# Moving three of the weight loads of an attention kernel's last stage, and its last store, to ScalarE's DMA queue

## The chip, the cores and the metric

One core of one Trainium2 chip. The time is the device time of one execution in microseconds. Nearly all executions of this kernel agree within 0.1%; a run counts as fast when it is within 1.5% of the fastest of its kernel. The profile is of one execution; its span, from the first to the last instruction, is about 1.8 us shorter than the timed figure.

Some words used below. A load has landed when all 16 DMA engines have reported their share of it. The granted clock is the share of TensorE's full clock that the trace records; "half clock" means a record of 0.5. An eviction copies a result of TensorE from PSUM, where matmuls leave it, to SBUF, the memory that the engines work from. A head is one of the 32 slices of wo that the output projection multiplies in turn. Times within an execution count from the first instruction of its profile.

## The reference

Grouped-query attention over a cache, for 32 sequences of 4 new tokens, with an output projection:

```python
B, Sq, D = 32, 4, 1024;  Hq, Hkv, Sk, Dh = 32, 4, 2048, 128
q = (x @ wq).reshape(B, Sq, Hq, Dh).transpose(0, 2, 1, 3)
k = repeat(k_cache, 8, axis=1);  v = repeat(v_cache, 8, axis=1)      # each 32 x 2 MiB, bf16
p = softmax(einsum("bhqd,bhkd->bhqk", q, k) * Dh ** -0.5)
o = einsum("bhqk,bhkd->bhqd", p, v)
return o.transpose(0, 2, 1, 3).reshape(B, Sq, Hq * Dh) @ wo          # wo: 4096 x 1024, 8 MiB
```

The kernel reads 151 MB and writes 0.26 MB.

## The kernel before

The kernel goes through 32 batches. All loads are issued by SyncE, in one order fixed at build time: x, four parts of wq, then k and v of the batches, then wo. Each load waits for the work that frees its slot. wo (32 heads, each 128 x 1024) comes in 14 pieces: six of 4 heads (1 MiB), two of 2, two of 1, and four halves of the last two heads.

```python
WO = (4, 4, 4, 4, 4, 4, 2, 2, 1, 1)          # heads in each piece; the last two heads come in halves
...
wo_for = [("k", B - 3), ("k", B - 2), ("k", B - 1), ("v", B - 4)]     # whose slots wo takes
...
for c, (u, m, n0, n1) in enumerate(pieces):
    ...
    p.dma("sp", lambda e, dst=dst, src=src: e.dma_start(dst, src),
        [("kt", b, 1) if kind == "k" else ("pv", b)], ("wo", c), f"s_wo{c}")
```

Every engine's program is a list in program order, so an engine's DMA issue stands between its other instructions. ScalarE's last work is the evictions of the attention output, one a batch (`o_evac`), and a third of the last copy:

```python
for i in range(B + LAG):
    j = i - LAG
    ...
    if j >= 0:
        for t in range(T):
            pe_pv(j, t)          # TensorE: attention of batch j
        ...
        o_evac(j)                # ScalarE: PSUM -> SBUF
    ...
for b0, n in ((0, 30), (30, 1), (31, 1)):
    o_turn(b0, n)                # VectorE: transpose the attention output
for u in range(Hq - 2):
    oproj(u, (0, 1, 2))          # TensorE: head u, waits for its piece of wo
...
oproj_out()                      # casts on VectorE, ScalarE, VectorE; two stores
```

## Time and profile before

| | before |
|---|---|
| time, median | 363.12 us |
| DMA queue of SyncE, share of the 16 engines | 99.0% |
| the six large loads of wo landed at | 340.6, 343.1, 345.5, 348.0, 350.5, 353.0 us |
| output projection, start of the first to end of the last matmul | 342.85 to 358.65 us |
| last piece of wo landed at | 358.2 us |

Here are lines of the page: the span, the table of DMA queues (packets, MB, share of the 16 engines' span), and the chain that ended last, by engine and by line.

```profile
span 361.4 us, 6252 instructions
...
q1 hardware_dynamic: 12240, 151.52, 99.0%
...
DMA 8%; PE 2%; SPq 1%; DVE 0%; issue 0%
DMA big<-in_wo_dram 8%; PE ps_r L394 1%; PE ps_s L420 1%; PE ps_s L16 1%; SPq L227 1%; DVE P_sb L434 0%; SPq L211 0%
```

One queue keeps the engines full, and the chain that ends last leads back to a load of wo. The chain of waits in order of time (start, duration, what) says which one:

```profile
325.16 27.84 DMA big<-in_wo_dram
...
353.04 0.39 PE ps_s L420
...
358.04 1.04 DVE P_sb L434 x2
```

A load lands at 353.0 and TensorE then works without a gap to the casts. Which load that is shows in the loads taken one by one (issue durations in ns and start of the issue; then the time from issue to landing). The first pair is the second load of wo, the second pair the sixth:

```profile
L227 SPq DMA_DIRECT2D big<-in_wo_dram x1: 432/432/432, 323.3 to 323.3; - x1
...
DMA to landing us min/median/max: 19.8/19.8/19.8
...
L227 SPq DMA_DIRECT2D big<-in_wo_dram x1: 433/433/433, 325.2 to 325.2; - x1
...
DMA to landing us min/median/max: 27.8/27.8/27.8
```

So the second load was issued at 323.3 and landed at 343.1; the sixth was issued at 325.2 and landed at 353.0. The stretches of 2 us (busy time of each engine, granted TensorE clock, DMA share, GB/s) show the stage:

```profile
core 0: us, PE busy (x) PEld busy (x) DVE busy (x) ACT busy (x) POOL busy (x), PEclk, DMA share, GB/s
...
344.00:346.00 2.00, 2.00 (x16) 0.49 (x5) 0.00 (x0) 0.00 (x0) 0.00 (x0) 1.00 0.99 410
346.00:348.00 2.00, 2.00 (x16) 0.39 (x4) 0.00 (x0) 0.00 (x0) 0.00 (x0) 1.00 1.02 426
...
350.00:352.00 2.00, 1.45 (x10) 0.39 (x4) 0.00 (x0) 0.00 (x0) 0.00 (x0) 1.00 1.00 412
352.00:354.00 2.00, 1.42 (x11) 0.29 (x3) 0.00 (x0) 0.00 (x0) 0.00 (x0) 1.00 1.00 395
...
356.00:358.00 2.00, 2.00 (x15) 0.55 (x6) 0.00 (x0) 0.00 (x0) 0.00 (x0) 1.00 0.42 144
```

TensorE starts the projection at 342.85, is full from 344 until it has caught up with the loads, and has holes at 350 to 354, where it waits for the fifth and the sixth. The DMA share falls only after 356.

### The profile page before, as it was taken

Reading aid. Unit: us, or ns where it says so; the run is one execution under the profiler, and the core shown is the slowest. Engines: PE = TensorE matmul, PEld = TensorE weight load, DVE = VectorE, ACT = ScalarE, POOL = GpSimd, SP = SyncE. Lnnn points to the kernel's source line nnn. Section 1 sums busy time; section 2 is a strip of 40 time slices with the busy share of each in tenths; the row PEclk is TensorE's granted clock in tenths of the full one; section 3 lists DMA queues with packets and bytes.
Section 4 is the critical chain, followed back from the end, with each engine's and each line's share of the span. In section 5 each row is a group of like instructions: output and inputs, shape, how many; then the busy total and the mean of one; then the engine's idle time right before and its main releaser. Section 6 shows DMA issues by size and latency. Waiting matters only on the chain. (4 is left out here: it accounts for less than half of the span.)

```text
span 361.4 us, 6252 instructions
## 1 busy us (share of the span) xinstructions
PE 307.8 (85%) x3034; PEld 147.0 (41%) x2340; DVE 269.4 (75%) x171; ACT 102.6 (28%) x110; POOL 165.4 (46%) x262
## 2 busy tenths in 40 slices
PE   1988788999989999988999888888888898889896
PEld 1002000444444555444444444443333444449711
DVE  0018799999899888879999888888888888866501
ACT  1014222333333333333333333323222233333000
POOL 8002055255555555554455444445555554444000
PEclk9999999999999999999999999999999999999999
DMA  8999999999999999999999999999999999999995
GB/s 321 433 435 432 424 424 428 435 423 424 423 428 432 428 424 430 431 430 426 424 433 428 425 428 430 430 428 426 428 432 432 426 423 435 428 426 428 413 415 215
DMA packets 12251, 151.66 MB, mean 420 GB/s; under 512 B 1360, under 2 KB 2128, under 8 KB 2768
## 3 DMA queue, kind: packets, MB, share of 16 engines
q1 hardware_dynamic: 12240, 151.52, 99.0%
q8 instruction: 6, 0.10, 0.1%
q14 instruction: 5, 0.04, 0.0%
HBM read 151.26 MB, written 0.26 MB: 419 GB/s over the span
## 5 line engine op out<-in xcount | busy, mean ns | idle before, releaser
L328 DVE STREAM_TRANSPOSE KT_sb<-big 128x2048 f32<-128x2048 f32 x64 | 146.6, 2293 | 16.7 <-DMA big<-in_k_cache_dram 16.7
L354 ACT ACTIVATE P_sb<-ps_s,negmx 128x2048 bf16<-128x2048 f32 x32 | 82.1, 2565 | 185.0 <-DVE negmx L350 185.0
L16 PE MATMUL ps_s<-KT_sb,QD_sb 128*128 128x512 bf16 x384 | 103.7, 377 | 0.0
L385 POOL COPY PD_sb<-PT_sb 32x1024 f32<-32x1024 f32 x62 | 64.1, 1034 | 63.3 <-PE ps_r L394 60.4
L385 POOL COPY big<-PT_sb 32x1024 f32<-32x1024 f32 x61 | 63.1, 1034 | 59.1 <-PE ps_r L394 56.3
L350 DVE TENSOR_REDUCE negmx<-ps_s 128x1 f32<-128x2048 f32 x32 | 73.2, 2286 | 12.4 <-PE ps_s L16 10.7
L394 PE MATMUL ps_r<-big 128*128 128x128 bf16 x1024 | 59.8, 219 | 11.4 <-PEq L85 11.4
L394 PE MATMUL ps_r<-big,PD_sb 128*128 128x128 bf16 x1024 | 59.8, 219 | 9.9 <-PEq L85 9.8
L394 PEld LDWEIGHTS ps_r<-big 128*128 128x128 bf16 x1024 | 57.9, 98 | 22.1 <-issue 21.6
L394 PEld LDWEIGHTS ps_r<-big,PD_sb 128*128 128x128 bf16 x1024 | 58.0, 98 | 21.1 <-issue 20.6
L341 PE MATMUL ps_s<-KT_sb,QD_sb 128*128 128x512 bf16 x128 | 48.3, 377 | 18.4 <-PEq L85 18.4
L341 PEld LDWEIGHTS ps_s<-KT_sb,QD_sb 128*128 128x128 bf16 x128 | 12.3, 96 | 103.1 <-issue 103.1
L363 DVE STREAM_TRANSPOSE PT_sb<-P_sb 128x1024 f32<-128x1024 f32 x32 | 39.8, 1245 | 15.8 <-ACT P_sb L354 15.8
L318 POOL COPY QD_sb<-QT_sb 32x64 f32<-32x64 f32 x128 | 29.4, 230 | 46.2 <-DVE QT_sb L297 20.5
L16 PE MATMUL ps_r<-ident 128*128 128x384 bf16 x173 | 33.3, 325 | 0.0
L366 PEld LDWEIGHTS ps_r<-ssum,permf 128*128 128x128 f32 x64 | 11.9, 187 | 24.8 <-issue 23.1
L403 ACT ACTIVATE QT_sb<-ps_r,rinv 128x128 bf16<-128x128 f32 x32 | 11.8, 367 | 29.4 <-PE ps_r L394 27.2
L279 DVE TENSOR_SCALAR KT_sb<-ps_r 128x512 bf16<-128x512 f32 x2 | 1.3, 684 | 20.3 <-PE ps_r L263 20.3
L420 PE MATMUL ps_s<-big,KT_sb 128*128 128x512 bf16 (+1 forms) x34 | 12.5, 375 | 2.0 <-DMA big<-in_wo_dram 1.2
L434 DVE CAST P_sb<-ps_s 128x512 bf16<-128x512 f32 (+1 forms) x2 | 1.0, 542 | 15.3 <-PE ps_s L420 15.3
L16 PE MATMUL ps_s<-big,KT_sb 128*128 128x224 bf16 (+1 forms) x62 | 12.0, 272 | 0.0
L252 PE MATMUL ps_r<-ident 128*128 128x384 bf16 x32 | 10.3, 322 | 0.0
(41 smaller groups left out, 85.8 us busy)
## 6 DMA issues: line engine op xcount, KB each, us to landing
big<-in_k_cache_dram SPq DMA_DIRECT2D x32, 2048.0 KB, 18.6
big<-in_v_cache_dram SPq DMA_DIRECT2D x32, 2048.0 KB, 22.1
big<-in_wq_dram SPq DMA_DIRECT2D x4, 2048.0 KB, 14.0
big<-in_wo_dram SPq DMA_DIRECT2D x6, 1024.0 KB, 22.8
big<-in_wo_dram SPq DMA_DIRECT2D x2, 512.0 KB, 24.3
big<-in_wo_dram SPq DMA_DIRECT2D x2, 256.0 KB, 22.6
big<-in_wo_dram SPq DMA_DIRECT2D x4, 128.0 KB, 17.5
P_sb<-in_x_dram SPq DMA_DIRECT2D x1, 256.0 KB, 2.6
```

What stands on the lines that cost most here:

```text
L16: return eng.add_instruction(mybir.InstMatmult(name=nc.get_next_instruction_name(), engine=eng.engine, start_tensor_calc=start, stop_tenso ...
L318: p.op("pool", lambda e, s=src, d=dst: e.tensor_copy(d, s), waits if g == 0 else [("pt", i - 2)] * (g == 1 and i > 1), ("qd", i) if g == G ...
L328: p.op("dve", lambda e, s=src, d=dst: e.transpose(d, s), waits, ("kt", i, c), gives="t_kt" if c else None)
L341: mm = lambda e, a_=(out_, lhsT, rhs), f=first, l=last: e.matmul(a_[0], lhsT=a_[1], rhs=a_[2], start=f, stop=l, skip_group_check=True)
L350: p.op("dve", lambda e: e.tensor_reduce(negmx[:, i % 4:i % 4 + 1], ps_s[:, :], AX.X, ALU.max, negate=True), [("qk", i)], ("negmx", i))
L354: p.op("act", lambda e: e.activation(P_sb[:, :, :, :].rearrange("p t r w -> p t w r"), ps_s[:, :].rearrange("p (t w r) -> p t w r", w=2, r=R),
L363: p.op("dve", lambda e: e.transpose(dst, src), [("exp", i)], ("pt", i))
L366: p.op("pe", lambda e: e.matmul(ring[(i if i == L else i // 2 * 2) % 4][:, 510 + i % 2:511 + i % 2], lhsT=permf[:, :], rhs=ssum[:, i % 4:i ...
L385: p.op("dve" if i >= B - 2 and g < i - B + 4 else "pool", lambda e, s=src, d=dst: e.tensor_copy(d, s), [free] * (g == 0 or i >= B - 2) + [ ...
L394: p.op("pe", lambda e: e.matmul(buf[:, 0:Dh], lhsT=pd_of(i)[:, t // 2, :, :, :, t % 2].rearrange("p x g q -> p (x g q)"), rhs=big[:, slot_ ...
L403: p.op("act", lambda e: e.activation(dst, src, ACT.Copy, scale=rinv[:, i % 4:i % 4 + 1]), [("pv", i), ("rinv", i)], ("o", i))
L420: mm = lambda e, a=(out_, lhsT, rhs): e.matmul(a[0], lhsT=a[1], rhs=a[2], start=(u == 0), stop=(u == Hq - 1), skip_group_check=True)
```

## The change

The intent: let a second sequencer issue part of the last loads, beside the others, and issue the two stores from two engines.

```diff
+        act_loads = []
         for c, (u, m, n0, n1) in enumerate(pieces):
 ...
-            p.dma("sp", lambda e, dst=dst, src=src: e.dma_start(dst, src),
-                [("kt", b, 1) if kind == "k" else ("pv", b)], ("wo", c), f"s_wo{c}")
+            load = ("act" if c in (1, 3, 5) else "sp", lambda e, dst=dst, src=src: e.dma_start(dst, src),
+                    [("kt", b, 1) if kind == "k" else ("pv", b)], ("wo", c), f"s_wo{c}")
+            if c in (1, 3, 5):
+                act_loads.append(load)
+            else:
+                p.dma(*load)
 ...
-                p.dma("sp", lambda e, n0=n0, n1=n1: e.dma_start(out_flat[:, n0:n1], y_sb[:, n0:n1]),
+                p.dma(("sp", "act")[j], lambda e, n0=n0, n1=n1: e.dma_start(out_flat[:, n0:n1], y_sb[:, n0:n1]),
 ...
                 o_evac(j)
+                if j == L - 1:
+                    for load in act_loads:
+                        p.dma(*load)
```

L is 31, so the three loads stand in ScalarE's program after the eviction of batch 30 and before that of batch 31.

## The prediction

> **What bounds the kernel now.** The loads. The queue table has one busy queue with 99.0% of the 16 engines' span; in the table of stretches the DMA share is 0.94 to 1.04 from 300 to 356 us, at 410 to 433 GB/s (395 and 368 at 352 to 356). So all 151 MB come one after the other. TensorE (85%) follows.
>
> The last stage, from the stretches, the timeline and the wo loads taken stretch by stretch: SyncE issues the six 1 MiB loads of wo at 322.8 to 325.2 us behind the last v load, and they land in order at 340.6, 343.1, 345.5, 348.0, 350.5 and 353.0, 2.45 us apart. The output projection starts at 342.85 (after the last transpose), runs 0.435 us for each of 32 heads, catches up with the loads at about 348 and then waits for the fifth and the sixth load (0.57 and 0.58 us). The chain of waits ends: sixth load lands 353.0, then TensorE without a gap to 358.56, casts, stores, 361.4. So the end is the landing of the sixth load plus 5.5 us. The last small pieces land at about 358.1 to 358.2, which is a second floor only 0.3 us below.
>
> **What the change does.** ScalarE's program has its three loads after the eviction of batch 30, which ran at 337.76 to 338.13, and before that of 31 (342.00). So loads 2, 4, 6 are issued at about 338.2 to 339.5 (0.43 us each, as SyncE's) instead of 323.3 to 325.2. SyncE's queue loses 3 MiB. SyncE's issues after 330.8 are today stretched to 1.2 to 6.3 us[...]; they get shorter, which is worth nothing, as these pieces were queued long before they moved.
>
> The Trainium skill, "DMA: Bandwidth & Descriptors", section "Issuing engines are not separate DMA queues", says that DMAs of all issuers run on the same 16 engines and only issue time is saved. This trace fits: engines full with one queue. Its section "Queues, rings and completion order" says that an engine takes turns between queues by packet; this trace cannot show it, having one busy queue. If so, from about 339.4 (issue plus about 1 us) both queues share 0.40 MiB/us. Estimate, equal shares: loads 1, 3, 5 land at 341.7, 346.7, 351.8; loads 2, 4, 6 at 344.4, 349.4, 353.8 to 354.4 (the earlier if ScalarE's 8 KB packets gain against SyncE's 4 KB ones). Total bytes and the end of the drain stay. Load 6 is then 0.8 to 1.4 us later, and the end follows it.
>
> The last store: ScalarE's part of the last eviction ends at 359.00, VectorE's at 359.08; SyncE issued its second store at about 359.17. ScalarE can issue at about 359.1: under 0.1 us gained.
>
> **Prediction.** 363.12 + 0.9 - 0.1 = 363.9 us; 8 in 10: 362.9 to 365.0. Faster by over 2%: 0.01; within 2%: 0.97; slower: 0.02.
>
> **What would show it.** A second queue with about 3 MB; its three issues at about 338 to 340; odd and even loads landing interleaved, the sixth at about 354; TensorE waits for loads 3 to 6 grown from 1.2 us to over 2; the drain's end unmoved; GB/s unmoved before 338.
>
> **What would make it wrong.** Two queues move more than one (each 1% of this stage is 0.2 us): slightly faster. ScalarE gets more than half: the sixth load is not late, time unchanged. ScalarE's issue blocked behind SyncE's stretched ones: the eviction of 31 and the projection start late, 1 to 3 us more. A gap in the engines' work about 333 to 339, if SyncE's queue ran empty: it holds 5 MiB then, so I expect none.

## More of the kernel before

The output projection takes the heads in order, so it needs the pieces of wo in order. The kernel also has `pe_idle(n, ...)`, which issues n matmuls whose result nobody reads, to keep TensorE busy in waits.

## The result

| | before | changed |
|---|---|---|
| median of 6 runs | 363.13 us (363.01 to 363.27) | 366.54 us (365.57 to 366.79) |
| span of the profiled run | 361.4 us | 364.7 us |
| granted TensorE clock, mean | 1.0 | 0.995 in five of six runs, 1.0 in the one of 365.57 us |
| wo, loads 1, 3, 5 landed at | 340.6, 345.5, 350.5 | 340.3, 344.0, 349.0 us |
| wo, loads 2, 4, 6 landed at | 343.1, 348.0, 353.0 | 347.8, 351.6, 355.3 us |
| last piece of wo landed at | 358.2 | 357.9 us |

The ratio is 1.0089, with a 95% interval of 1.0076 to 1.0102. A ratio here is the mean time of one kernel's fast runs over that of the other's of the same rounds, so it is not quite the ratio of the medians. By the 2% class the two are the same; but the 3.4 us are clear of the noise, and the 366.54 us lie above the prediction's range (362.9 to 365.0).

The same lines of the page, after:

```profile
span 364.7 us, 6248 instructions
...
q1 hardware_dynamic: 11664, 148.25, 95.9%
q10 hardware_dynamic: 576, 3.28, 2.2%
...
PE 9%; DMA 3%; DVE 0%; DVEq 0%; issue 0%; ACT 0%
```

The second queue is there, with 3.28 MB (three loads and a store). The chain now ends in TensorE's own work (9%) and less in DMA (3%). In order of time:

```profile
337.44 10.36 DMA big<-in_wo_dram
...
347.85 0.39 PE ps_s L425
...
348.56 0.43 PE ps_s L425
348.98 0.43 PE ps_s L16 x2
```

The load that starts the last chain is issued at 337.44 and lands at 347.80. ScalarE's loads one by one are the second load of wo (first pair) and the sixth (second pair):

```profile
L228 ACTq DMA_DIRECT2D big<-in_wo_dram x1: 402/402/402, 337.4 to 337.4; - x1
...
DMA to landing us min/median/max: 10.4/10.4/10.4
...
L228 ACTq DMA_DIRECT2D big<-in_wo_dram x1: 452/452/452, 338.4 to 338.4; - x1
...
DMA to landing us min/median/max: 16.9/16.9/16.9
```

The second load is issued at 337.4 and lands 10.4 us later, at 347.8. From there TensorE has 28 of 32 heads still to do. Its matmuls come at half the pace at first: a group of three column blocks takes 0.85 us (348.56 to 349.41) and not 0.43. The timeline shows the wait, in brackets at the end of the line:

```profile
start us, us, engine line op out<-in xcount [idle before <-releaser]
...
337.44 1.37 ACTq L228 DMA_DIRECT2D big<-in_wo_dram  x3
...
347.85 0.39 PE L425 MATMUL ps_s<-big,KT_sb 128*128 128x512 bf16 x1 [3.25 <-DMA big<-in_wo_dram]
```

The ScalarE issue of 337.44 to 338.81 runs beside the eviction and delays nothing. TensorE's projection starts at the same time as before to within 0.2 us, does the four heads of the first load, and waits 3.25 us. The stretches:

```profile
core 0: us, PE busy (x) PEld busy (x) DVE busy (x) ACT busy (x) POOL busy (x), PEclk, DMA share, GB/s
...
344.00:346.00 2.00, 0.60 (x5) 0.00 (x1) 0.00 (x0) 0.00 (x0) 0.00 (x0) 1.00 1.00 412
346.00:348.00 2.00, 0.15 (x1) 0.10 (x1) 0.00 (x0) 0.00 (x0) 0.00 (x0) 1.00 1.02 424
348.00:350.00 2.00, 2.00 (x9) 0.40 (x3) 0.00 (x0) 0.00 (x0) 0.00 (x0) 0.56 1.00 412
350.00:352.00 2.00, 2.00 (x10) 0.31 (x3) 0.00 (x0) 0.00 (x0) 0.00 (x0) 0.59 1.02 420
...
356.00:358.00 2.00, 2.00 (x15) 0.45 (x5) 0.00 (x0) 0.00 (x0) 0.00 (x0) 1.00 0.42 145
```

From 344 to 348 TensorE does 0.75 us of work. From 348 to 352 (whose TensorE columns are full only because each matmul takes longer) its granted clock is 0.56 and 0.59; the trace has one record of 0.5, from 348.2 to 351.6 us. The DMA columns have not changed: the GB/s of each stretch are within 10 of those before, and the engines run dry at the same time. So the bytes did not come later. They came in another order.

The trace's records of single DMA packets show how the queues shared the engines. By queue, in stretches of 1 us of the changed kernel:

```
us     SyncE's queue       ScalarE's queue
340    56 packets 400 KB    1 packet     8 KB
341    24 packets 176 KB   31 packets  248 KB
342    28 packets 200 KB   25 packets  200 KB
352    35 packets 110 KB   36 packets  288 KB
354   211 packets 354 KB    6 packets   16 KB
```

ScalarE's first packet starts at 341.00, and sixteen of them have started by 341.4. The first is 3.56 us after its issue began. From then on, as long as ScalarE's queue has packets for all engines (to about 352 us), the two queues have about the same number of packets, also where their packets differ in size (352 us), so the engines take turns by packet. The Trainium skill says so ("DMA: Bandwidth & Descriptors", section "Queues, rings and completion order"), and this trace agrees.

### The profile page after: what moved, and what is told of

It is laid out like the page before. It is cut to its first block, busy times and chain, and to the rows that moved or that the text cites. A ratio compares the mean times of both kernels' runs of the same rounds, so it can differ in the third digit from the quotient of the medians.

```text
span 364.7 us, 6248 instructions
## 1 busy us (share of the span) xinstructions
PE 308.2 (85%) x3030; PEld 147.2 (40%) x2340; DVE 269.5 (74%) x171; ACT 102.6 (28%) x110; POOL 165.3 (45%) x262
## 3 DMA queue, kind: packets, MB, share of 16 engines
q10 hardware_dynamic: 576, 3.28, 2.2%
## 5 line engine op out<-in xcount | busy, mean ns | idle before, releaser
L16 PE MATMUL ps_s<-big,KT_sb 128*128 128x224 bf16 (+1 forms) x62 | 12.9, 291 | 1.2 <-DVE KT_sb L415 1.1
```

The source lines that it names most:

```text
L16: return eng.add_instruction(mybir.InstMatmult(name=nc.get_next_instruction_name(), engine=eng.engine, start_tensor_calc=start, stop_tenso ...
```

## The experiments

Two theories of the 3.56 us from ScalarE's issue to its first packet were open. In the changed kernel SyncE has an issue under way from 337.54 to 341.21 us, stretched from the usual 0.43 us, and it ends when ScalarE's packets start. Theory A: ScalarE's loads stand behind that issue. Theory B: it has another cause (B1 the first use of the queue, B2 a fixed delay on busy engines, B3 a fixed number of SyncE's packets that go first).

### Only the loads, or only the store

```diff
 loads_only, against the changed kernel
-                p.dma(("sp", "act")[j], ...           # stores
+                p.dma("sp", ...
 store_only, against the kernel before
-                p.dma("sp", ...                       # stores
+                p.dma(("sp", "act")[j], ...
```

Expected of loads_only:

> The three loads on ScalarE's queue, both stores on SyncE's. Both theories (A and B below) lay the whole loss on the loads: time as the changed kernel's, 366.5 us, at most 0.1 us above it; the second load lands at about 347.8 us and TensorE waits 3.3 us for it. If the store on ScalarE's queue cost something, this run is faster than 366.3.

Expected of store_only:

> Only the last store on ScalarE's queue. Expected 363.1 us, at most 0.1 us below before (the second store is issued about 0.06 us earlier). Anything over 363.5 would mean that the second queue itself costs time.

Measured: loads_only 366.69 us (365.40 to 367.83), ratio 1.0109 (1.0092 to 1.0126). store_only 363.01 us (363.00 to 363.08), ratio 0.9997 (0.9981 to 1.0014). The whole loss is the loads (the median is 0.1 us above what was expected, well within the spread of the four runs). The store is worth about 0.1 us by the medians, which its interval does not separate from nothing. The four runs of loads_only had mean clocks of 1.0 (the fastest, 365.40), 0.995 twice and 0.991 (the slowest, 367.83): the half clock comes in some executions and not in others. A mean of 0.995 is what one stretch of 3.41 us at half clock makes of it, and 0.991 what two would make; the run with 0.991 has no profile.

### Filling TensorE's wait

```diff
 fill, against the changed kernel
         for u in range(Hq - 2):
+            if u == WO[0]:                            # head 4, the first of the second load
+                pe_idle(18, ring[0][:, 0:IDLE], idle_rhs)
             oproj(u, (0, 1, 2))
```

> The changed kernel, with 18 idle matmuls (about 2.9 us of TensorE work) put between head 3 and head 4 of the output projection, where TensorE waits 3.3 us for the second load. If the half clock from 348.2 to 351.6 us is a consequence of that wait, the clock stays at 1.0 and the time falls by 1.4 to 1.7 us, to about 365.0. If the half clock has another cause, time and clock stay at 366.5 and 0.995.

Measured: 365.63 us (365.40 to 366.43), ratio 1.0076 (1.006 to 1.0093), and the clock was 1.0 in all four runs. In the timeline the last idle matmuls end, the second load comes, and head 4 follows at full speed:

```profile
346.27 1.30 PE L16 MATMUL ps_r<-ident 128*128 128x384 bf16 x7
...
347.93 0.39 PE L425 MATMUL ps_s<-big,KT_sb 128*128 128x512 bf16 x1 [0.36 <-DMA big<-in_wo_dram]
348.15 0.38 PE L16 MATMUL ps_s<-big,KT_sb 128*128 128x288 bf16 x2
...
348.37 0.38 PE L425 MATMUL ps_s<-big,KT_sb 128*128 128x512 bf16 x1
```

The heads come 0.44 us apart again (347.93 to 348.37). The half clock is a consequence of the wait: with the wait filled, it came in none of four runs here and in none of four of order_sp_fill below, against five of six and three of four. The filling gave back about 0.9 us of the median and not the expected 1.4 to 1.7. The reason is in the landings of this run: with the clock full, the sixth load binds next. It landed at 355.30, and 12 heads of 0.435 us end at 360.5. One of the four runs (366.43) was slow with a full clock; I have no profile of it. Neither kernel beats the one before.

### No stretched issue on SyncE

```diff
 hold, against the changed kernel
-                    [("kt", b, 1) if kind == "k" else ("pv", b)], ("wo", c), f"s_wo{c}")
+                    [("kt", b, 1) if kind == "k" else ("pv", b)] + [("o", B - 1)] * (c >= 10), ("wo", c), f"s_wo{c}")
```

> The changed kernel, with SyncE's last four small loads held until the last eviction (about 342.2 us), so that SyncE has no stretched issue under way when ScalarE issues at 337.4. Theory A (ScalarE's loads are held behind SyncE's stretched issue of 337.54 to 341.21 us): the first packet of ScalarE's queue starts at about 338.5 to 339 instead of 341.0, the second load lands at about 345, TensorE waits under 1 us for it, the clock stays full, time 363.7 to 364.6. Theory B (the 3.1 us from issue to first packet come from SyncE's packets already handed to the engines, or from the queue's first use): first packet at 341, second load at 347.8, time 366.5.

Measured: 366.72 us (366.56 to 367.82), ratio 1.0109. ScalarE's issue began at 337.71, when SyncE had no issue under way: its last one before had ended at 332.1, and its four held ones came at 342.34.

```profile
337.71 0.87 ACTq L228 DMA_DIRECT2D big<-in_wo_dram  x2
...
342.34 2.94 SPq L228 DMA_DIRECT2D big<-in_wo_dram  x4
```

The first packet came at 341.22, which is 3.51 us after the issue (the 3.1 us of the expectation should have read 3.56). The second load landed at 347.8. Theory A, which was my first, falls.

### Small loads in the middle of the kernel

```diff
 probe, against the changed kernel
+        probe = sbuf("probe", [128, 3, 256], BF16)
 ...
+                if j in (5, 13, 21):
+                    n = j // 8
+                    p.dma("act", lambda e, n=n: e.dma_start(probe[:, n, :], x_flat[:, 256 * n:256 * (n + 1)]), [], ("probe", n), f"s_p{n}")
```

(The end of the kernel also waits for the three loads.)

> The changed kernel, with three small extra loads (64 KB of x into a scratch tile) on ScalarE's queue after the evictions of batches 5, 13 and 21, while SyncE's queue moves k and v in 16 KB packets. Measured is the time from the start of the issue to the first packet of ScalarE's queue. Theory B1 (first use of the queue is slow): over 3 us for the first small load, about 1 us for the second and third and for the second load of wo, which then lands at about 345. Theory B2 (a fixed delay of a new queue on busy engines): about 3.5 us for all of them. Theory B3 (a fixed number of SyncE's packets goes first, 12 or 13 of 0.28 us at 337 us): 7 us or more among packets of 0.615 us. Time about 367, as 0.2 MB are added and nothing is mended.

Measured, from the records of single packets:

```
issue begins   first packet of ScalarE's queue   delay      SyncE's packets meanwhile
114.08 us      117.52 us                         3.44 us    k, v, 16 KB
186.84         190.29                            3.45       k, v, 16 KB
264.07         267.54                            3.47       k, v, 16 KB
338.38         341.85                            3.47       wo, 8 KB
363.20         364.07                            0.87       the first store, 1 KB, from 363.69 on
```

The time was 367.21 us in the one run. B1 and B3 fall, and B2 fits: the delay is about 3.45 us on the first use of the queue and the fourth, and among packets that take 0.615 us each (16 KB) as well as among those of 0.31 us (8 KB; the 0.28 us of the expectation is a mean with tiny records in it). A rival is left: a fixed number of SyncE's bytes that go first, about 1.4 MB, would look the same, as the engines moved about 400 to 440 GB/s in all these stretches; no run tests it. With engines that were idle at the issue the delay is 0.87 us; SyncE's very first load (x, issued at 0.74, first packet at 1.77 in the changed kernel) has 1.03 us, and 1.16 in probe. What the 2.5 us more are spent on, no run here shows; they were seen only for a queue that starts beside a busy one.

### The same loads issued earlier

```diff
 early, against the changed kernel              early2: L - 3
-                if j == L - 1:
+                if j == L - 2:
```

Expected of early:

> The changed kernel with the three loads one eviction earlier on ScalarE (about 334.0 us instead of 337.4). If the loss comes from the second load being late by its start delay and half rate: first packet at about 337.5, second load lands at about 344.4, TensorE waits under 0.5 us for it, no half clock, later waits for loads 4 and 6 at about 350 and 354; time 363.5 to 364.5. If the loss belongs to two queues sharing the engines, whatever the moment: 366 or more.

Expected of early2:

> Two evictions earlier (about 330.6 us): first packet at about 334.2, where v of batch 31 is being loaded. Turns by packet let 8 KB of wo pass for every 16 KB of v, so the last v load lands about 2 us later (340 instead of 338), attention of batch 31 and the output projection start about 2 us later (345), and TensorE then needs 13.9 us without waits: end of the projection about 359, time 363.3 to 364.5. If the engines serve one queue first, the last v load lands unmoved at 338 or over 3 us late.

Measured: early 364.69 us (364.66 to 364.71), ratio 1.0044; early2 365.06 us (364.94 to 365.10), ratio 1.0054. Mean clocks were 1.0, but for one run of early2 with 0.995.

In early, ScalarE's issue began at 333.84, its first packet came at 337.32 (3.48 us), and the second load landed at 343.5. That is more than half of the loss won back, with two queues as before; about half of the gain is the half clock that did not come, as the changed kernel's one run without it took 365.57. It is 0.2 us over the expected range, because ScalarE's packets now took turns with the first load too: SyncE's loads 1, 3, 5 landed at 343.2, 348.2 and 352.9. The waits for wo in early (total us, times, longest) are several short ones in place of one of 3.25 us:

```profile
PEld ps_s L425 <- DMA big<-in_wo_dram: 4.8, 3, 1.9
...
PE ps_s L425 <- DMA big<-in_wo_dram: 2.3, 2, 1.3
PE ps_s L16 <- DMA big<-in_wo_dram: 1.4, 1, 1.4
```

In early2 the last v load landed at 339.7 instead of 337.9, and the projection started about 2 us later, as expected of turns by packet. The time is 0.6 us above the expected range: SyncE's third load came at 349.6 and held TensorE up once more, which I had not worked out.

### Only the fourth and the sixth load

```diff
 fourth_sixth, against the changed kernel
-            if c in (1, 3, 5):                        # twice
+            if c in (3, 5):
```

> Only the fourth and the sixth load on ScalarE's queue, at the same moment as in the changed kernel. Same start delay and same sharing, but the load that comes late is not the one that TensorE needs next: second load (SyncE) at about 344, third at about 349, fourth at about 347.8, fifth at about 353, sixth at about 351.6. TensorE waits about 2.7 us for the third load (perhaps with the half clock after it), little later. Time 363.2 to 364.0 without the half clock, up to 365 with it. If any load on ScalarE's queue costs as in the changed kernel: 366.5.

Measured: 366.14 us (365.72 to 366.37), ratio 1.008, with a mean clock of 0.994 or 0.995 in all four runs. The landings of the loads that were waited for were as expected (third load 349.4, fourth 348.0, fifth 352.8); the sixth came at 352.8, 1.2 us later than expected, and bound nothing. TensorE waited 3.0 us for the third, with the half clock after it. My expected time missed by 1.1 us, and my own landings show it: the third load left 24 heads to do, so the projection could not end before 349.4 + 24 x 0.435 = 359.8, which is 1.6 us later than in the kernel before and so about 364.7 us without the half clock, against the 363.2 to 364.0 that I expected.

### A late second load without a second queue

```diff
 order_sp, against the kernel before
-        for c, (u, m, n0, n1) in enumerate(pieces):
+        for c in (0, 2, 3, 1) + tuple(range(4, len(pieces))):
+            u, m, n0, n1 = pieces[c]
 order_sp_fill: the same, with the 18 idle matmuls of fill
```

Expected of order_sp:

> The kernel before, all loads on SyncE's queue, but issued in the order 1, 3, 4, 2, 5, 6: the second load lands fourth, at about 348.0 us, as late as in the changed kernel, with no second queue. If the loss is the lateness of the load that TensorE needs next: TensorE waits about 3.4 us for it, the half clock follows, and 28 heads from 348.0 take 12.2 us and 1.7 us more: end of the projection about 361.9, time 366.3 to 366.8. If two queues as such cost the time: 363.1 to 363.5.

Expected of order_sp_fill:

> The same with 18 idle matmuls before head 4. Clock full; 28 heads from 348.0 end at about 360.2; the sixth load lands at 353.0 as in the kernel before and binds nothing: time 364.6 to 365.1, so 1.7 us less than the run without the idle matmuls (in the changed kernel they gave back less, as its sixth load, landing at 355.3, bound next). If the idle matmuls do not keep the clock here: as the other run.

Measured: order_sp 366.48 us (365.08 to 366.67), ratio 1.0094; order_sp_fill 365.17 us (364.99 to 365.23), ratio 1.0057, 0.07 us above its range. With one queue and one load out of order the kernel loses what the changed kernel loses. The profiled run of order_sp was the one of its four with a full clock (365.08; the others had 0.995 and 366.45 to 366.67). Its timeline shows that a wait of 3.32 us does not always bring the half clock (nor did one of 3.22 us in the profiled run of loads_only):

```profile
347.99 0.39 PE L421 MATMUL ps_s<-big,KT_sb 128*128 128x512 bf16 x1 [3.32 <-DMA big<-in_wo_dram]
```

### One sum for all of them

TensorE cannot end before any load's landing plus the heads from that load on, at 0.435 us each. The load with the largest sum binds. Half clock for 3.4 us adds 1.7 us to the sum of the load whose wait it follows. All landings are those of the profiled runs:

| kernel | binding load, landed | heads left | sum | half clock | over before's 358.2 | span over before's |
|---|---|---|---|---|---|---|
| before | sixth, 353.0 | 12 | 358.2 | no | | |
| changed | second, 347.8 | 28 | 360.0 | yes | 3.5 | 3.3 |
| hold | second, 347.8 | 28 | 360.0 | yes | 3.5 | 3.4 |
| fill | sixth, 355.3 | 12 | 360.5 | no | 2.3 | 2.2 |
| loads_only (profiled run) | sixth, 355.2 | 12 | 360.4 | no | 2.2 | 2.2 |
| early | fifth, 352.9 | 16 | 359.8 | no | 1.6 | 1.5 |
| early2 | third, 349.6 | 24 | 360.1 | no | 1.9 | 1.7 |
| fourth_sixth | third, 349.4 | 24 | 359.8 | yes | 3.3 | 3.2 |
| order_sp (profiled run) | second, 347.9 | 28 | 360.1 | no | 1.9 | 1.9 |
| order_sp_fill | second, 347.8 | 28 | 360.0 | no | 1.8 | 1.8 |

The sum holds within 0.2 us for all nine. In the changed kernel the second load binds only with the half clock after it (360.0 + 1.7 = 361.7); without the half clock the sixth does (355.3 + 12 x 0.435 = 360.5), as in fill and in the profiled run of loads_only.

No version beats the kernel before beyond noise, and the sum says why: its loads land in the order in which they are needed, its sixth load binds at 358.2, and the engines deliver the last byte at 358.2. By this sum, another order can only make some load later.

## Why the prediction was wrong

1. **What bounds the kernel: right.** The engines are full, and the drain of wo ended at 357.9 after and 358.2 before.
2. **The second queue takes turns by packet and adds no bandwidth: right**, shown by about equal packet counts and unchanged GB/s. The Trainium skill ("DMA: Bandwidth & Descriptors", section "Issuing engines are not separate DMA queues") was the right thing to rest on.
3. **The failed step: "from about 339.4 (issue plus about 1 us) both queues share", and so "loads 2, 4, 6 at 344.4, 349.4, 353.8 to 354.4".** They landed at 347.8, 351.6 and 355.3. For the second load the 3.4 us are: issue 0.8 us earlier than I took it (337.4: it did not wait for the eviction beside it, which itself ran 0.3 us earlier than in the kernel before); 3.56 us from issue to first packet where I had allowed about 1.2, which puts the first packet at 341.0 and not at 339.4; 5.1 us at half rate up to the first engine's landing (346.1), where I had 5.0; and 1.7 us from the first of the 16 engines to the last (347.8), which I had left out. Start delay and spread are the two mis-sized terms, about 1.6 and 1.7 us net.
4. **"Load 6 is then 0.8 to 1.4 us later, and the end follows it": too small, and not the only load that could bind.** Load 6 came 2.3 us later (355.3 against 353.0). The prediction's own sum, 363.12 + 2.3 - 0.1 = 365.3, is then near the runs without the half clock (365.57 here, 365.40 in loads_only), where load 6 does bind. What it did not look at is the second load. My own figures had it at 344.4 and TensorE ready for it at 342.85 + 4 x 0.435 = 344.6. It had 0.2 us to spare and 28 heads behind it. Over three microseconds late, it alone asks for an end of 360.0, only 0.5 us before the 360.5 of the sixth, and with the half clock that its wait brings it binds, at 361.7. order_sp, where the sixth load came in time (352.9), shows that this lateness alone is enough.
5. **The half clock: not foreseen.** The wait of 3.25 us was followed by 3.4 us at a clock of 0.5. The Trainium skill has this ("TensorE: Matmul & The Clock Gate", section "Part 1: The HAM clock gate (the "warmup" mystery)"): the clock falls to half after an idle window of about 3.4 us, and the windows run freely, without regard to when the kernel starts, so a wait can hit or miss. The runs agree: it hit five of six runs of the changed kernel and three of four of order_sp. The traces show more. Their clock records, but for the last that the end cuts off, are all whole multiples of 3.41 us long, so windows of 3.41 us can be counted on from the first. In the four profiled runs with the half clock (changed, hold, probe, fourth_sixth), the window just before it held 0.2 to 0.9 us of matmuls. In the two with a wait of over 3 us and the full clock (3.22 us in loads_only, 3.32 us in order_sp), the wait was split between two windows, and each still held 1.7 to 1.9 us. In these six, then, it was where the wait fell, and not its length, that decided. All twelve profiles fit: each of their 16 falls to the half clock (12 of them after the last matmul, where they cost nothing) ends a window with at most 1.2 us of matmuls, and every other window held at least 1.5 us. The net cost is the distance between runs with and without it, about 1.0 us in the changed kernel (366.5 against 365.6) and 1.4 to 1.6 in order_sp (366.45 to 366.67 against 365.08); the full 1.7 does not show in the changed kernel, as its sixth load binds next.
6. **The store: not contradicted.** About 0.1 us by store_only, not separated from nothing.
7. **SyncE's stretched issues worth nothing: right** for the time; hold also cleared them of blocking ScalarE. What stretches them, no run tested.

## What to carry to other kernels

With the DMA engines full, as here, the second queue changed the order in which the bytes arrived and not their rate, so put down for each load when it lands and how much work stands behind it; the load with the largest sum sets the end, and it need not be the last. On the single queue here, loads that were issued long before landed 2.45 us apart with no start-up time between them, whereas the load put on another queue late paid its start delay (3.5 us on busy engines), then moved at half the rate. A wait of about 3 us, which brought the half clock in most runs here, should be filled or avoided, as its cost comes on top and differs from run to run.

## What the Trainium skill lacked or had wrong

- "DMA: Bandwidth & Descriptors", section "Latency and other measured facts", gives about 600 ns to the first byte for loads issued by SyncE and ScalarE. With engines that were idle at the issue this agrees roughly: 0.87 to 1.16 us from the start of an issue that itself takes 0.35 to 0.38. The page has no figure for a queue that starts while another keeps the engines full: 3.44 to 3.58 us here, in every one of the eleven cases looked at, whatever the packet size (8 or 16 KB) and whether first use or not. Why it is longer stays open.
- The same page's section "Where 436 GB/s comes from" says that for HBM to SBUF the HBM side (about 358 GB/s) binds. The same paragraph also gives 425 GB/s for a load of 16 MB. This one-core kernel moved 413 to 435 GB/s in 38 of the 40 equal slices of its span. The page "Perfetto Trace Analysis", section "Engine Utilization", has it right.
- No page that I read gives a figure for the spread between the 16 engines of one load: the first engine's share of a 1 MiB load landed 2.1 us before the last one's in the kernel before (338.5 and 340.6 us), and 3.9 us before it in early, where two queues took turns.
- "TensorE: Matmul & The Clock Gate", section "Why this matters for your kernels", warns of gaps over about 3 us. The runs agree and add that the length of the gap does not settle it: waits of 3.0 and 3.25 us brought the half clock, and those of 3.22 us (loads_only) and 3.32 us (order_sp) did not. What settles it in the twelve profiles is the matmul time in one window of 3.41 us: with up to 1.2 us of it the clock fell, with 1.5 us or more it did not. So the window need not be wholly idle; where between 1.2 and 1.5 us the limit lies, no run shows.
